# A new hand-written order of all engines: first-layer weights in whole quarters, and 53 fills of 256 columns

## The chip, the cores and the metric

One Trainium2 chip, and one of its cores. A core has a tensor engine (PE; its weight loads are listed apart as PEld), a vector engine (DVE), a scalar engine (ACT), a pool engine (POOL) and a sync engine whose queue (SP) issues all DMAs of this kernel. The metric is the device time of one execution in microseconds, lower is better. The kernel before took 179.84 us, the median of 179.12, 179.84 and 180.20.

## The reference

A gated linear recurrence over 768 steps for 4 batches and 8 heads of 48 dimensions, and behind it two dense layers over the 3072 tokens.

```python
f = 1 / (1 + exp(-f_logit))
for t in range(S):                                   # S = 768
    state = f[:, :, t, :, None] * state + einsum('bhd,bhe->bhde', k[:, :, t], v[:, :, t])
    y[:, :, t] = einsum('bhd,bhde->bhe', q[:, :, t], state)
x = y.transpose(0, 2, 1, 3).reshape(3072, 384)
h = x @ w_in                                         # 384 x 2048
out = maximum(0.01 * h, h) @ w_out                   # 2048 x 384
```

## The kernel before, in words

The sequence is cut into chunks of 128 steps. The work comes in 12 units: units 0 to 3 hold chunks 0 and 1 of one batch each, and units 4 to 11 hold one later chunk of two batches each. `a` is the half of a unit (a group of heads in units 0 to 3, a batch in the others; 2 means both).

A unit runs through the parts below. The names are the words of the order, `name_unit_a`, and the last number of some words names the engine (0 DVE, 1 ACT or POOL, 2 POOL).

- `Lf Lk Lq Lv` load f_logit, k, q and v on SP's queue. `ge` (line 229) takes an exponential of the gate logits on ACT and `gl` (line 241) the logarithm, which gives `lf`.
- `cs` (lines 250 to 261) makes the cumulative sums of `lf` with matmuls against triangular masks; `ca` (line 266, DVE) finishes them for two units. `dec` (lines 274 to 280, ACT) turns them into the three decay factors `em`, `at` and `end`.
- `k` and `q` (line 286) scale the keys and queries, and `v` (lines 291 to 300, POOL) casts the values. `tk tq` transpose on PE (line 319) and `ck cq` copy the result out (lines 332, 334); from unit 3 on `xk xq` transpose by DMA instead (line 339).
- `sc` (lines 355, 362) makes the scores, `mk` (lines 372, 376, DVE) masks them, and `mx` and `ms` (line 393) mix values and states into the output. `xt` (lines 445, 447) copies that into `xT`, the input of the first layer.
- `pt` (lines 458, 463) makes a chunk's contribution to the state, `sf` (lines 473, 475, DVE) adds it, and `sb` (lines 480, 483, POOL) scales and casts the state.
- `up` (line 510, for one unit, 6 matmuls of 256 columns) and `uw` (line 521, for two units, 3 matmuls of 512 columns) are the first layer; `pr` and `pw` (lines 516, 525, ACT) its leaky relu into `gT`. `dn` (line 532, 4 matmuls of 384 columns) is a quarter of the second layer for 128 tokens; `dh` (line 548) is the same layer for half of the columns. `ob` and `oh` copy out, `st` and `sh` store.

The weights come as four quarters each. `WI_i` (line 173) loads 512 columns of the first layer's weights into a staging tile, and `CI_i_x` (lines 200, 202) casts one of its three slices of contraction rows. `We_i_x` (line 180) loads only 256 of the columns, and `Ce_i_x_y` (lines 187, 189) casts 128 of those. `WO` and `CO` do the same for the second layer. The staging tiles are the raw tiles of units 4 and 5, and a `WO_i` uses the staging tile of `WI_i`.

`F_n@b` (line 134) issues n matmuls of a constant tile into PSUM bank b. Nothing reads them.

Nothing is scheduled by a compiler. The string `order` near the end lists every part with the PSUM banks it uses, and each engine and the queue run their own words in the order of that string. There are 8 banks, so a word on PE also waits until the reader of the bank's last contents is done.

Of the kernel before, what the change touches and what calls it, by code (L numbers as in the profile page):

```python
# [15 lines left out]
def kernel(  # L16
# [10 lines left out]
    nc = tc.nc  # L27
# [53 lines left out]
    banks = [psum.tile([128, 512], FP32, name=f"ps{i}", tag=f"ps{i}") for i in range(8)]  # L81
# [4 lines left out]
    ut = const.tile([128, 128], BF16, tag="ut")  # L86
# [3 lines left out]
    filler = const.tile([128, 128], BF16, tag="filler")  # L90
# [41 lines left out]
    def fill(n, bank):  # L132
        for _ in range(n):
            nc.tensor.matmul(banks[bank].rearrange("t (a n) -> t a n", a=4), filler,  # L134
                             filler[:, None, :].to_broadcast([128, 4, 128]), start=True, stop=True)
# [349 lines left out]
    def wide(j):  # L485
        return j // 2 * 2 in WIDE
# [101 lines left out]
    sc_0_0@6.2 q_1_1_1 zv_1_1 mk_0_0_0 gl_2_1 F_2@1 cs_2_1@3 q_1_0_0 ca_2_1 F_1@4 tq_1_0@1 dec_2_0 ck_1_0_0 cq_1_0_1
    mk_0_0_1 tq_1_1@4 We_0_0 q_2_0_0 cq_1_1_1 v_1_0 dec_2_1 Lv_2_2 WI_2 F_2@5 sc_1_0@6.7 mx_0_2@5.1 sc_1_1@2.4
    mk_1_0_1 mk_1_0_0 v_1_1 tq_2_0@7 q_2_1_1 mk_1_1_1 mk_1_1_0 xt_0_0_1 ms_0 pt_1_2@3.6 xt_0_1_1 Ce_0_1_0_1  # L590
    Ce_0_1_1_1 F_2@2 mx_1_2@5.4 k_2_0_0 tk_2_0@1 sf_1_0 cq_2_0_0 Ce_0_0_0_1 Ce_0_0_1_1 xt_1_0_1 up_0_1@2 k_2_1_1
    ck_2_0_0 sb_1_0 tq_2_1@3 tk_2_1@7 sf_0_1 v_2_1 v_2_0 We_1_0 up_0_0@1 cq_2_1_1 CI_2_1_2 zs_2_1 ms_1 pr_0_1
    xt_1_1_1 ut Ce_1_0_0_2 ck_2_1_0 sc_2_0@5.0 sc_2_1@3.7 sf_1_1 pr_0_0 mk_2_1_0 CI_2_0_1 pt_2_2@2.6 CI_2_2_0
    up_1_1@4 mk_2_0_1 sf_2_0 up_1_0@1 mk_2_1_1 Ce_1_0_1_1 pr_1_1 pr_1_0 mk_2_0_0 up_0_5@3 up_1_5@0 We_1_1 Lf_3_2
    sb_2_0 WI_3 up_1_4@2 up_0_2@4 mx_2_2@7.1 WO_0 CI_3_1_2 ms_2 xt_2_1_0 Ce_1_1_1_0 xt_2_0_1 up_1_2@5 up_0_4@7
    Ce_1_1_0_0 pr_1_5 pr_1_2 WO_2 pr_1_4 CI_3_2_2 zs_3_0 ge_3_0 pr_0_2 WO_1 up_0_3@1 ge_3_1 CI_3_0_0 up_2_3@0
    up_2_1@5 up_1_3@2 pr_0_3 sf_2_1 up_1_6@4 gl_3_0 pr_1_3 up_0_6@6 up_2_0@1 pr_0_5 CO_0_1_0 CO_0_2_0 pr_2_3 up_2_2@2
    up_2_7@3 sb_0_1 cs_3_0@0 CO_0_0_2 CO_2_1_2 pr_0_4 CO_2_0_2 gl_3_1 CO_1_2_2 Lf_4_1 CO_1_0_2 pr_2_1 pr_2_2 pr_0_6
    ca_3_0 cs_3_1@7 dec_3_0 pr_2_7 pr_1_6 dn_0_1_0@5 up_2_4@2 up_1_7@6 dn_0_0_0@0 up_2_6@3 Lk_3_2 dn_1_0_0@4 CO_1_1_2
    Lf_5_1 pr_2_4 k_3_0_0 CO_2_2_0 ca_3_1 dec_3_1 Lq_3_2 Lf_5_0 WO_3 dn_0_0_1 q_3_1_1 pr_2_6 CO_3_1_0 k_3_1_1 Lf_4_0  # L600
    dn_1_0_1 dn_1_0_2 dn_0_1_1 dn_1_1_0@2 dn_0_0_2 Lv_3_2 dn_1_1_1 xk_3 sb_1_1 pr_1_7 dn_1_1_2 up_2_5@7 q_3_0_0
    dn_0_1_2 up_0_7@3 CO_3_0_0 v_3_0 sb_2_1 CO_3_2_1 pr_0_7 xq_3 Lq_4_0 v_3_1 Lk_4_0 Lq_5_1 Lk_5_1 Lk_5_0 Lq_5_0
# [78 lines left out]
```

## Time and profile before

| | us |
|---|---|
| median of three runs | 179.84 |
| the profiled execution, its own time | 178.5 |
| its span, first to last instruction | 176.7 |
| its last matmul ends at | 173.8 |
| PE busy | 168.0 |
| ACT busy | 107.5 |
| DVE busy | 79.1 |
| POOL busy | 72.7 |

Times in the text count from the start of the span. The profile of an engine says when an instruction ran, and what ended the idle time before it. A matmul's listed duration holds its latency; in a row of matmuls the next one starts earlier, so what a group costs PE is read from the chain of waits, which lists starts and merged lengths.

### The profile page before, as it was taken

To read this page: it belongs to the slowest core of one execution; us is meant where nothing else is said; L and a number is where in the kernel's file an instruction comes from. 1 tells how busy PE (TensorE), PEld (TensorE's weight loads), DVE (VectorE), ACT (ScalarE), POOL (GpSimd) and SP (SyncE) were. 2 spreads that over 40 slices of the span, in tenths; PEclk is the share of its full clock that TensorE was granted. 3 is DMA by queue.
4 is the path that set the end of the run, shared out by engine and by line. 5 is a ranking of instruction groups with operands and counts; after the bars stand their busy time and mean duration, and the time that the engine had idled before them with its cause. 6 is when DMAs were issued, how large, how long until landed. Compare 5 with 4: busy or idle time off the path is not lost.

```text
span 176.7 us, 5136 instructions
## 1 busy us (share of the span) xinstructions
PE 168.0 (95%) x2096; PEld 105.6 (60%) x2096; DVE 79.1 (45%) x166; ACT 107.5 (61%) x234; POOL 72.7 (41%) x151
## 2 busy tenths in 40 slices
PE   7698889999999999999999998999999999999993
PEld 2475668787566786754556744455754555644662
DVE  5259957802217333835128844506735355300030
ACT  4886964999155599269960687641799610378401
POOL 4687585532551745208525344802206980000000
PEclk9999999999999999999999999999999999999999
DMA  5999999499999499979999889999999990103004
GB/s 148 317 323 342 355 312 353 125 326 209 312 206 210 91 194 177 215 188 200 211 229 233 192 188 216 227 134 212 264 206 225 156 250 0 48 0 137 0 22 156
DMA packets 110407, 34.93 MB, mean 198 GB/s; under 512 B 102832, under 2 KB 109616, under 8 KB 110384
## 3 DMA queue, kind: packets, MB, share of 16 engines
q1 hardware_dynamic: 110384, 34.61, 84.1%
q8 instruction: 16, 0.26, 0.6%
q14 instruction: 7, 0.06, 0.1%
HBM read 25.17 MB, written 4.72 MB: 169 GB/s over the span
## 4 chain that ended last, share of the span: by engine, by line
PE 90%; DVE 3%; ACT 2%; DMA 2%; issue 1%; SPq 0%; DVEq 0%
PE ps L532 35%; PE ps L521 22%; PE ps L510 11%; PE ps L393 6%; PE ps L134 3%; PE ps L362 3%; DMA raw_fk<-in_f_logit_dram 2%; PE ps L319 2%; PE ps L548 2%; PE ps L258 1%; DVE wm L372 1%; PE ps L463 1%; PE ps L355 1%; PE ps L458 1%; PE ps L250 1%
## 5 line engine op out<-in xcount | busy, mean ns | idle before, releaser
L532 PE MATMUL ps<-w_out,gT 128*128 128x384 bf16 x368 | 66.1, 326 | 0.9 <-DVE sf L475 0.9
L532 PEld LDWEIGHTS <-gT 128*128 128x128 bf16 x368 | 34.4, 98 | 24.3 <-issue 1.2
L521 PE MATMUL ps<-xT,w_in 128*128 128x512 bf16 x192 | 45.2, 379 | 0.0
L525 ACT ACTIVATE gT<-ps 128x512 bf16<-128x512 f32 x64 | 34.5, 623 | 10.1 <-PE ps L521 9.6
L521 PEld LDWEIGHTS <-w_in 128*128 128x128 bf16 x192 | 18.1, 98 | 18.9
L376 DVE TENSOR_TENSOR wm<-ps,ut 128x512 bf16<-128x512 f32 x32 | 19.9, 684 | 17.0 <-PE ps L362 12.2
L286 POOL TENSOR_TENSOR qh<-raw_qv,at 128x768 bf16<-128x768 f32 (+1 forms) x10 | 14.0, 1404 | 24.3 <-ACT gT L525 9.4
L510 PE MATMUL ps<-xT,w_in 128*128 128x256 bf16 x192 | 22.9, 273 | 0.4 <-ACT xT L445 0.2
L516 ACT ACTIVATE gT<-ps 128x512 bf16<-128x512 f32 x32 | 17.9, 616 | 6.2 <-PE ps L510 6.2
L291 POOL CAST vb<-raw_qv 128x384 bf16<-128x384 f32 (+1 forms) x16 | 11.6, 723 | 23.6 <-DMA raw_qv<-in_v_dram 23.4
L510 PEld LDWEIGHTS <-w_in 128*128 128x128 bf16 x192 | 18.4, 98 | 3.6 <-DVE w_in L189 0.5
L483 POOL CAST sb<-sf 64x192 bf16<-64x192 f32 x40 | 14.9, 374 | 10.8 <-DVE sf L473 8.5
L445 ACT CAST xT<-ps 128x384 bf16<-128x384 f32 x15 | 7.8, 529 | 16.9 <-PE ps L393 13.5
L274 ACT ACTIVATE em<-ps 128x384 bf16<-128x384 f32 x24 | 12.2, 508 | 9.0 <-DVE wm L376 5.5
L229 ACT ACTIVATE e<-raw_fk 128x384 f32<-128x384 f32 (+1 forms) x16 | 11.0, 685 | 8.1 <-DMA raw_fk<-in_f_logit_dram 8.0
L286 DVE TENSOR_TENSOR kh<-raw_fk,em 128x768 bf16<-128x768 f32 (+1 forms) x10 | 9.0, 901 | 14.6 <-ACT em L274 9.7
L475 DVE TENSOR_TENSOR sf<-sf,ps 64x192 f32<-64x192 f32 x32 | 11.2, 351 | 6.4 <-ACT at L275 2.8
L543 DVE COPY osb<-ps 128x384 f32<-128x384 f32 x13 | 7.1, 554 | 13.0 <-PE ps L532 9.0
L275 ACT ACTIVATE at<-ps 128x384 bf16<-128x384 f32 x24 | 12.3, 512 | 0.0
L480 POOL TENSOR_TENSOR sf<-sf,end 128x192 f32<-128x192 f32 x16 | 8.9, 556 | 5.9 <-DVE sf L475 5.6
L372 DVE TENSOR_TENSOR wm<-ps,pair_mask 128x512 bf16<-128x512 f32 x16 | 10.4, 685 | 1.8 <-ACT lf L241 0.9
L134 PE MATMUL ps<-filler 128*128 128x512 bf16 x24 | 9.2, 511 | 2.0 <-DVE filler L93 1.1
(90 smaller groups left out, 180.2 us busy)
## 6 DMA issues: line engine op xcount, KB each, us to landing
out_dram<-osb SPq DMA_DIRECT2D x23, 192.0 KB, 3.1
raw_fk<-in_f_logit_dram SPq DMA_DIRECT2D x18, 192.0 KB, 3.8
raw_qv<-in_v_dram SPq DMA_DIRECT2D x18, 192.0 KB, 3.6
raw_fk<-in_k_dram SPq DMA_DIRECT2D x18, 192.0 KB, 3.7
raw_qv<-in_q_dram SPq DMA_DIRECT2D x18, 192.0 KB, 3.8
raw_fk<-in_moe_w_out_dram SPq DMA_DIRECT2D x2, 768.0 KB, 7.2
raw_qv<-in_moe_w_out_dram SPq DMA_DIRECT2D x2, 768.0 KB, 5.0
raw_fk<-in_f_logit_dram SPq DMA_DIRECT2D x3, 384.0 KB, 4.7
```

The costliest lines, as they stand in the source:

```text
L134: nc.tensor.matmul(banks[bank].rearrange("t (a n) -> t a n", a=4), filler, filler[:, None, :].to_broadcast([128, 4, 128]), start=True, sto ...
L274: nc.scalar.activation(ems[j % 2][:, a], t[:, 0:H * D], AF.Exp, scale=1.0)
L275: nc.scalar.activation(ats[j % 2][:, a], t[:, 0:H * D], AF.Exp, scale=-1.0)
L286: eng.tensor_mul(heads(j, to[j % NR], a)[:, :, :, 0:D], raw_heads(j, x, a), decays(j, by, a))
L372: nc.vector.tensor_mul(w.rearrange("t (s p) n -> t s p n", s=2), src.rearrange("t (s p n) -> t s p n", s=2, p=2), pair_mask[:, :, None, :] ...
L376: nc.vector.tensor_mul(w, src.rearrange("t (p n) -> t p n", p=P2), ut[:, None, :].to_broadcast([128, P2, 128]))
L483: nc.gpsimd.tensor_copy(out=sb[rows, :, y * D:y * D + D], in_=sf[rows])
L510: nc.tensor.matmul(pm[:, i, :], w_in_of(ff, kk), xTs[j // 2 % 2][:, kk, j % 2].rearrange("t a s -> t (a s)"), start=(kk == 0), stop=(kk == ...
L516: nc.scalar.activation(dst, pm, AF.Prelu, alpha=0.01)
L521: nc.tensor.matmul(banks[bank], w_in_of(ff, kk), xTs[j // 2 % 2][:, kk].rearrange("t u a s -> t (u a s)"), start=(kk == 0), stop=(kk == NK ...
L525: nc.scalar.activation(g_blocks(j)[ff], banks[st[j].pop(("pm", ff))], AF.Prelu, alpha=0.01)
L532: nc.tensor.matmul(po, g_of(j, ff, a), w_out_b[quarter][:, ff % 4, :], start=(ff == 0), stop=(ff == NF - 1))
```

## The change

Three things change. The fill matmul has 256 columns instead of 512. The order string is another one from its first line to its last, so all engines and SP's queue run their words in a new sequence, with other banks. Some parts change their engine or their form: the first-layer weights are loaded as `WI_0` to `WI_3` and cast by `CI` (four loads of 768 KB, where there were two of these and four `We` of half the size), and 11 places in the order hold 53 fills, where 8 places held 24. All other matmuls are the same ones as before.

```diff
     def fill(n, bank):
         for _ in range(n):
-            nc.tensor.matmul(banks[bank].rearrange("t (a n) -> t a n", a=4), filler,
-                             filler[:, None, :].to_broadcast([128, 4, 128]), start=True, stop=True)
+            nc.tensor.matmul(banks[bank][:, 0:256].rearrange("t (a n) -> t a n", a=2), filler,
+                             filler[:, None, :].to_broadcast([128, 2, 128]), start=True, stop=True)
...
     order = """
-    c0 Lf_0_1 ge_0_1 Lf_1_2 ge_1_1 gl_0_1 ge_1_0 zk_0 zv_0_0 zs_0_0 Lv_0_1 Lf_0_0 F_7@1 cs_0_1@0 ge_0_0 gl_0_0 Lk_0_1
+    c0 Lf_0_1 zs_1_1 zk_2 ge_0_1 zk_0 Lk_0_1 Lf_0_0 Lq_0_0 Lf_1_2 Lk_0_0 Lq_0_1 gl_0_1 F_16@1 cs_0_1@0 zs_0_1 ge_0_0
...
```

PE's words in the new order, as far as the first two `up`, are `F_16@1 cs_0_1 F_1@2 cs_0_0 F_19@3 cs_1_0 tq_0_1 tk_0_1 cs_1_1 tk_0_0 tq_0_0 F_1@3 sc_0_1 tq_1_0 F_1@6 sc_0_0 pt_0 tk_1_0 F_4@1 tq_1_1 sc_1_0 tk_1_1 cs_2_0 F_2@6 sc_1_1 F_3@1 pt_1 cs_2_1 mx_0 F_2@4 mx_1 ms_0 ms_1 cs_3_1 cs_3_0 up_0_1 tq_2_0 up_0_0`. Behind them come `F_1@5` and `F_3@4` between ups. Before, PE began with `F_7@1 cs_0_1 F_3@2 cs_0_0 F_3@3 cs_1_0`, and had four more fill places ahead of its second `mx`.

The first place is ACT at the start of the program. `e` is the exponential of one half of a unit's gate logits (line 229; tile 76 is unit 0, 77 is unit 1), `lf` its logarithm, and `em`, `at`, `end` are the decay factors. Before:

```order
L229 ACTIVATE e_76<-raw_fk_64 128x384
L229 ACTIVATE e_77<-raw_fk_65 128x384
L241 ACTIVATE lf_78<-e_76 128x4x2x48
L229 ACTIVATE e_77<-raw_fk_65 128x384
L229 ACTIVATE e_76<-raw_fk_64 128x384
L241 ACTIVATE lf_78<-e_76 128x4x2x48
L274 ACTIVATE em_87<-ps_155 128x384
```

Now:

```order
L229 ACTIVATE e_76<-raw_fk_64 128x384
L241 ACTIVATE lf_78<-e_76 128x4x2x48
L229 ACTIVATE e_76<-raw_fk_64 128x384
L241 ACTIVATE lf_78<-e_76 128x4x2x48
L274 ACTIVATE em_87<-ps_155 128x384
L275 ACTIVATE at_89<-ps_155 128x384
L277 ACTIVATE end_91<-ps_155 128x2x2
```

The logarithm of unit 0's first half stood behind an exponential of unit 1, which needs unit 1's load; now it follows its own exponential, and all of unit 0's gate stands ahead of unit 1.

The second place is SP's queue where the first-layer weights are loaded. `raw_fk_66` and `raw_qv_72` are unit 2, `raw_fk_67` is unit 3, and tiles 68, 69, 74 and 75 are the staging of quarters 0, 2, 1 and 3. Before:

```order
L164 DMA raw_fk_66<-in_k_dram 128x8x96
L180 DMA raw_fk_68<-in_moe_w_in_dram 128x3x256 x2
L164 DMA raw_qv_72<-in_v_dram 128x8x96
L173 DMA raw_fk_69<-in_moe_w_in_dram 128x3x512
L180 DMA raw_qv_74<-in_moe_w_in_dram 128x3x256 x2
L164 DMA raw_fk_67<-in_f_logit_dram 128x8x96
L173 DMA raw_qv_75<-in_moe_w_in_dram 128x3x512
```

Now:

```order
L164 DMA raw_fk_67<-in_f_logit_dram 128x8x96
L173 DMA raw_fk_68<-in_moe_w_in_dram 128x3x512
L164 DMA raw_qv_72<-in_q_dram 128x8x96
L173 DMA raw_fk_69<-in_moe_w_in_dram 128x3x512
L164 DMA raw_fk_66<-in_k_dram 128x8x96
L173 DMA raw_qv_74<-in_moe_w_in_dram 128x3x512
L173 DMA raw_qv_75<-in_moe_w_in_dram 128x3x512
L164 DMA raw_qv_72<-in_v_dram 128x8x96
```

Unit 3's gate logits moved ahead of all weights, and unit 2's q and k behind quarter 0 and quarter 2.

The third place is DVE between the masks of unit 2 and the state of unit 2 (`xT_126` is unit 2's input to the first layer, `w_in_172` is quarter 1, `sb` are state tiles being cleared). Before:

```order
L372 TENSOR_TENSOR wm_108<-ps_162,pair_mask 128x512
L372 TENSOR_TENSOR wm_105<-ps_160,pair_mask 128x512
L447 CAST xT_126<-ps_156 128x3x2x64
L189 CAST w_in_172<-raw_qv_74 128x3x128 x2
L127 MEMSET sb_0_123 128x192
```

Now:

```order
L123 MEMSET v_100 128x8x16
L334 COPY qT_103<-ps_159 128x2x256
L202 CAST w_in_172<-raw_qv_74 128x512
L334 COPY qT_103<-ps_158 128x2x256
L334 COPY kT_101<-ps_156 128x2x256
L334 COPY kT_101<-ps_162 128x2x256
L202 CAST w_in_174<-raw_qv_75 128x512
L372 TENSOR_TENSOR wm_105<-ps_162,pair_mask 128x512
```

The cast of quarter 1 stood behind unit 2's masks and behind the copy of unit 2's output; now it stands ahead of unit 2's masks.

More of the change, by code (lines that the diff above doesn't have):

```diff
@@ L588 @@
[L588 to L602, printed above, removed]
@@ new lines @@
+    cs_2_1@1 ca_2_1 ge_3_1 ge_3_0 sb_1_0 gl_3_1 gl_3_0 dec_2_0 CI_0_2_1 CI_0_0_2 mx_0_2@2.6 zs_2_0 xt_0_0_0 F_2@4
+    mx_1_2@4.5 ms_0 ms_1 cs_3_1@3 xt_0_1_1 dec_2_1 q_2_0_1 CI_0_1_0 cs_3_0@2 xt_1_0_0 xt_1_1_1 ca_3_1 up_0_1@6 pr_0_1
+    ca_3_0 tq_2_0@4 up_0_0@1 sf_0_1 up_1_1@5 WI_3 sf_1_1 CI_2_1_1 CI_2_2_0 ut dec_3_1 q_2_1_0 Lv_2_2 CI_2_0_2 k_2_1_0
+    up_1_0@7 up_1_5@6 up_0_5@0 k_2_0_0 zv_2_0 pr_0_0 pr_1_1 pr_0_5 CI_1_2_2 tq_2_1@3 cq_2_0_0 WO_0 pr_1_0 F_1@5
+    tk_2_1@1 up_0_4@5 up_1_4@0 Lk_3_2 tk_2_0@7 CI_1_1_1 dec_3_0 pr_1_5 CI_1_0_0 CI_3_2_2 cq_2_1_0 v_2_1 F_3@4
@@ L646 @@
+    sh_11_1_0
     """
```

103 lines of the change are left out of this document (56 added, 47 removed).

## The prediction

> **What bounds the kernel now.** I read the page first, then the busy time by stage, then the chain of waits.
>
> ```profile
> span 176.7 us, 5136 instructions
> PE 168.0 (95%) x2096; PEld 105.6 (60%) x2096; DVE 79.1 (45%) x166; ACT 107.5 (61%) x234; POOL 72.7 (41%) x151
> PE 90%; DVE 3%; ACT 2%; DMA 2%; issue 1%; SPq 0%; DVEq 0%
> ```
>
> PE is the bound: it has 90% of the chain. A gain can come only from holes on PE, from matmuls at a low rate and from fills. The stages show where those lie (stretch, length, busy us of PE, PEld, DVE, ACT, POOL, granted clock, DMA share, GB/s).
>
> ```profile
> 0.00:5.80 5.80, 3.17 (x8) 1.04 (x9) 2.40 (x15) 2.79 (x5) 2.25 (x17) 1.00 0.72 186
> 5.80:22.17 16.37, 15.02 (x338) 10.30 (x337) 12.47 (x27) 13.85 (x37) 12.62 (x31) 1.00 1.14 335
> 22.17:33.05 10.88, 10.02 (x208) 7.93 (x205) 7.26 (x18) 6.41 (x13) 7.51 (x21) 1.00 0.92 308
> 33.05:107.00 73.95, 73.95 (x905) 48.88 (x906) 32.90 (x67) 49.36 (x109) 31.95 (x53) 1.00 0.96 206
> 107.00:111.00 4.00, 3.08 (x21) 1.40 (x18) 1.81 (x4) 3.23 (x9) 1.24 (x4) 1.00 1.13 224
> 111.00:173.80 62.80, 62.76 (x627) 36.05 (x625) 22.29 (x38) 31.51 (x66) 17.14 (x28) 1.00 0.64 133
> ```
>
> From 33.05 to 173.80 PE has one hole, 0.92 us in the row 107 to 111. What else can be won lies ahead of 33 us. The chain of waits shows it (start, length, what).
>
> ```profile
> 1.26 3.53 DMA raw_fk<-in_f_logit_dram
> ...
> 5.33 0.42 ACT lf L241
> 5.80 0.32 PE ps L250
> 6.68 1.30 PE ps L134 x3
> 8.71 1.29 PE ps L134 x3
> ...
> 12.66 0.86 PE ps L134 x4
> ...
> 18.02 0.74 PE ps L393 x61
> ...
> 22.03 0.60 ACT xT L445
> ...
> 22.67 0.70 PE ps L510 x5
> ...
> 23.43 0.45 issue
> ...
> 31.59 0.28 DVE xT L447
> 31.88 0.21 issue
> 32.09 0.91 DVE w_in L189 x2
> 33.05 6.07 PE ps L510 x54
> ```
>
> The first real matmul waits until 5.80 for a logarithm that stands behind another unit's load. And matmuls run at half rate until about 9.8: a fill of 512 columns costs 0.43 us at 6.68 and 8.71 and 0.215 at 12.66, though the granted clock reads 1.00 throughout. A fill of 256 columns is put at 0.215 and 0.108 accordingly.
>
> **The start, up to the third cumulative sum.** ACT's prices are the distances from start to start in the timeline.
>
> ```profile
> 3.43 0.52 ACT L229 ACTIVATE e<-raw_fk 128x384 f32<-128x384 f32 x1 [1.42 <-DMA raw_fk<-in_f_logit_dram]
> 4.81 0.52 ACT L229 ACTIVATE e<-raw_fk 128x384 f32<-128x384 f32 x1 [0.86 <-DMA raw_fk<-in_f_logit_dram]
> 5.24 0.51 ACT L241 ACTIVATE lf<-e 128x384 bf16<-128x384 f32 x1
> 11.32 0.49 ACT L274 ACTIVATE em<-ps 128x384 bf16<-128x384 f32 x1
> 12.14 0.54 ACT L229 ACTIVATE e<-raw_fk 128x384 f32<-128x384 f32 x1
> 16.92 1.07 ACT L332 COPY qT<-ps 128x512 bf16<-128x512 bf16 x2 [0.74 <-PE ps L319]
> ...
> 35.88 2.06 ACT L516 ACTIVATE gT<-ps 128x512 bf16<-128x512 f32 x4 [0.34 <-PE ps L510]
> ```
>
> A gate step takes 0.43 (4.81 to 5.24), a set of decays 0.82 (11.32 to 12.14), a transposed copy 0.535, a relu 0.52. Unit 0's first load is not moved, so the exponential starts at 3.43 again; its logarithm now follows at 3.86 and ends at 4.37. The 16 fills last from 1.05 to 1.05 + 16 x 0.215 = 4.49, and `cs_0_1` starts there instead of at 5.80. The other half of unit 0 has 576 KB loaded up to and with it, as much as the load that ended at 4.79 before (1.26 + 3.53). Its logarithm ends near 5.75, and `cs_0_0` runs from 5.8 to 6.7 (0.88, as 5.80 to 6.68). F_19 then costs 19 x 0.108 = 2.05 at full rate, to 8.75, or 4.1 at half rate, to 10.8. ACT needs until about 9.4 for what follows `cs_0_0` (decays of unit 0's second half from 6.85, then four gate steps of unit 1), so at full rate F_19 fills a real wait and costs nothing. I take full rate from about 6.5 on, since PE is busy from 1.05 almost without a break, where before it stood still from 4.1 to 5.8 and the rate doubled some 4 us after that.
>
> [...]
>
> **Up to the first first-layer matmul.** From 9.4 on ACT's queue holds, ahead of the copy that completes unit 0's `xT`, three sets of decays, six copies, eight gate steps and one weight cast: 3 x 0.82 + 6 x 0.535 + 8 x 0.43 + 0.5 = 9.6, so 19.0 with no wait at all, and 19.6 with that copy (0.60). On PE the chain goes over POOL's cast of unit 1's values.
>
> ```profile
> 15.52 0.50 POOL L291 CAST vb<-raw_qv 128x384 bf16<-128x384 f32 x1 [0.77 <-DMA raw_qv<-in_v_dram]
> 16.65 0.50 POOL L291 CAST vb<-raw_qv 128x384 bf16<-128x384 f32 x1
> 21.41 0.81 POOL L483 CAST sb<-sf 64x192 bf16<-64x192 f32 x2 [0.76 <-DVE sf L473]
> ```
>
> Unit 1's values are the queue's 13th transfer now and were its 14th, with 384 KB less ahead of them, some 1.1 us at 335 GB/s. The load ended at 15.5, so now at 14.4. Two casts of 1.1 each (15.52 to 16.65) and the state cast of 0.8 between them end at 17.4. Then `pt_1` and `cs_2_1` (0.45 and 0.24 in the same chain view), both `mx` (0.74 each, the row at 18.02), two fills and `ms_0` (0.28) end at 20.1, and the copy at 20.7. This chain is the longer one; its ten handovers are counted at nothing and may cost up to 0.1 each, and its loads may be 0.3 earlier. I take the first `up` at 21.0, bounds 20.4 to 21.7, against 22.17. At that point PE has done 0.26 more: `ms_1` and both `cs_3` (0.28 and 2 x 0.24), less two transposes of unit 2 (2 x 0.25). Whole quarter 0 is 4608 KB into the queue, by 335 GB/s near 17, so its casts are not what is waited for. **Gain 1.4, bounds 0.7 to 2.0.**
>
> **From the first `up` to 33 us.** PE waited here from 22.17 to 22.67 but for one matmul of 0.1 (0.4), then 0.45, then from 31.59 to 33.05 (1.46): 2.3 in all. In the largest the copy of unit 2's output stood on DVE ahead of the two casts of quarter 1. That row of DVE is now ahead of unit 2's masks, and the cast follows the load. What it adds: four fills (0.43) among the ups, and waits of PE for banks, where ACT needs 14 x 0.52 for relus, 4 x 0.5 for casts and 2 x 0.82 for decays, 10.9 of some 13.5 us. I put these waits at 0.8, between 0.2 and 1.9. **Gain 2.3 - 0.43 - 0.8 = 1.1, bounds 0 to 1.7.**
>
> **Behind 33 us.** The order of everything else changes too, with the same matmuls. The one hole before was a bank that DVE's state addition had to free (columns as in the chain above).
>
> ```profile
> 110.08 0.34 DVE sf L475
> 110.46 0.37 DVE sf L475
> 110.87 0.81 PE ps L532 x4
> ```
>
> In the new order I find banks that come free only 0.1 to 0.5 us ahead of their next use, in each of the four wide units. I expect waits of about the same 0.9 us there: gain 0, bounds a gain of 0.9 and a loss of 3. The tail, two half layers and a store, is the same: nothing.
>
> **The sum.** -1.4 - 1.1 + 0 = -2.5 against the profiled execution's 178.5 (span 176.7 and 1.8 around it), so 176.0. That execution is 1.3 below the median; the same difference off the median gives **177.3**. With all bounds at their best it is 179.84 - 4.6 = 175.2, and at their worst 179.84 - 0.7 + 3 = 182.1.
>
> **Rivals.** (1) *The half rate lasts until 9.9 again.* F_19 then ends at 10.8, `cs_1_0` is 2.0 late, and ACT, which has unit 1's decays in front of all its copies, passes that on: -2.5 + 2.0, 179.3. For it speaks that this execution doubled only then; against it the pause before 5.80, which is gone.
>
> (2) *The middle is held by the loads.* The DMA share is 0.96 from 33 to 107 and 1.13 behind it. If loads cannot come earlier, PE's lead melts into waits: 179.8. Against it: the weights of the second layer wait for casts less often now, and the queue stood still for 4.9 and 3.6 us ahead of two of them.
>
> ```profile
> SPq L192 <- DVE w_in L189: 4.9, 1, 4.9
> SPq L192 <- DVE w_in L202: 3.6, 1, 3.6
> ```
>
> (3) *Slower: values behind the transposes.* On SP the values of units 6 and 7 stand behind unit 7's two DMA transposes, and POOL casts both in turn just ahead of PE's `mx_7`. Before, POOL waited longest of all for such loads, and PE's `mx` began at 98.4, with the second cast running.
>
> ```profile
> POOL vb L291 <- DMA raw_qv<-in_v_dram: 23.4, 8, 7.4
> 97.93 0.82 POOL L291 CAST vb<-raw_qv 128x768 bf16<-128x768 f32 x1 [1.32 <-DMA raw_qv<-in_v_dram]
> ```
>
> By my count of the queue the cast ends 0.8 us ahead of `mx_7` now. What the loads are late beyond that is lost one for one, since all ups of the pair wait for it. It makes the kernel slower from 0.8 + 2.5 + 0.9 = 4.2 us on; at 5.1 it is 181.6. The single wait of 7.4 shows that such a size occurs; that it never held PE before speaks against it.
>
> **Chances.** Forecast 0.60, (1) 0.12, (2) 0.08, (3) 0.20. A measurement can tell about 0.5% from no change, that is 178.9 to 180.7. The forecast lies below that, a third of (1) too: faster 0.64; the rest of (1) and (2) same: 0.14; (3) slower: 0.22, with a little of (2). The range is 175.0 to 181.4; the forecast's own is 175.2 to 178.9.
>
> **What would show it.** Right: the first line 250 matmul near 4.5, fills of 256 columns at 0.108 in the row of 19, the first line 510 matmul between 20.4 and 21.7, no wait of over 0.5 us for `w_in`, and PE busy through the rest but for 1 us. Wrong: the row of 19 fills lasting 4 us (1); the third `cs` waiting for a load; PE idle in front of line 393 with POOL's line 291 as the releaser (3), or more than 2 us of holes behind 33 us from ACT.

## The result: slower by 3.8%

| | before | after |
|---|---|---|
| median, us | 179.48 (178.87 to 180.20, 4 runs) | 184.99 (184.28 to 185.28, 4 runs) |
| the profiled execution | 178.5 | 185.28 |
| its span | 176.7 | 183.5 |
| its mean granted clock | 1.000 | 0.972 |

The ratio is 1.0382, with a 95% interval of 1.0328 to 1.0437. The forecast was 177.3, with a range of 175.0 to 181.4. Here and below, a ratio compares those executions of each kernel that lie within 1.5% of its fastest; a time given as measured is the median of all.

The page of the changed kernel first: the span, PE's busy time, the granted clock in 40 slices, and a DMA queue that the prediction never looked at (pieces, MB, share of the engines).

```profile
span 183.5 us, 5178 instructions
PE 171.7 (94%) x2125; PEld 110.2 (60%) x2125; DVE 84.4 (46%) x176; ACT 107.3 (58%) x233; POOL 68.4 (37%) x140
PEclk9999685899999999999999999999999999999999
q8 instruction: 16, 0.26, 0.5%
```

PE is busy 3.7 us longer than before, with only 29 matmuls more, and the clock row has a dent at 6, 8 and 5 where before it had 9 throughout. The busy time by stage shows where (columns as in the prediction).

```profile
10.00:15.00 5.00, 3.96 (x87) 2.88 (x85) 3.54 (x8) 4.04 (x12) 3.85 (x9) 1.00 1.05 285
15.00:20.00 5.00, 3.71 (x97) 2.62 (x105) 4.39 (x10) 4.49 (x11) 3.21 (x10) 0.97 0.97 301
20.00:25.00 5.00, 2.67 (x131) 1.68 (x109) 2.39 (x7) 1.09 (x4) 3.22 (x7) 0.69 1.08 368
25.00:30.00 5.00, 3.82 (x50) 2.88 (x50) 3.75 (x10) 3.14 (x8) 1.42 (x2) 0.66 1.07 371
30.00:35.00 5.00, 5.00 (x36) 3.83 (x35) 1.47 (x5) 2.18 (x6) 2.57 (x8) 0.66 0.87 286
35.00:107.00 72.00, 71.34 (x945) 48.03 (x946) 38.75 (x70) 43.97 (x94) 24.80 (x47) 1.00 0.98 189
107.00:180.40 73.40, 73.32 (x764) 42.04 (x752) 26.79 (x50) 41.47 (x88) 23.60 (x37) 1.00 0.67 146
```

Before, in the same three stretches from 20 us on:

```profile
20.00:25.00 5.00, 3.82 (x98) 2.64 (x92) 3.75 (x11) 3.31 (x8) 4.05 (x12) 1.00 1.03 315
25.00:30.00 5.00, 5.00 (x95) 4.33 (x95) 4.11 (x9) 3.35 (x7) 2.54 (x8) 1.00 1.01 360
30.00:35.00 5.00, 4.82 (x110) 3.80 (x109) 3.39 (x10) 3.80 (x9) 3.39 (x7) 1.00 0.57 159
```

Behind 35 us PE is full but for 0.7 us, so all of the loss lies ahead of it. Two things are new there: a stretch in which PE does little (2.67 of 5 us from 20 to 25), and a clock of 0.66 from 25 to 35. (The counts of 36 and 110 matmuls from 30 to 35 do not compare: 76 of the 110 are small ones of line 393.) What the clock costs is seen on rows of one kind: 30 first-layer matmuls take 5.42 us in the chain below, 0.18 each, and 54 took 6.07 before, 0.11 each. The chain of waits names the first.

```profile
18.54 0.51 POOL vb L291
19.09 0.35 PE ps L458 x8
19.79 1.06 PE ps L393 x54
20.84 0.54 PE ps L134 x2
21.39 1.29 PE ps L393 x63
22.67 2.49 issue
25.16 0.36 PE ps L393 x10
25.55 0.59 ACT xT L445
26.95 0.48 ACT xT L445
27.47 1.22 PE ps L510 x5
29.12 5.42 PE ps L510 x30
```

For 2.49 us in the middle of `ms_0` PE waits for "issue", that is, for nothing that the profile shows. In the chain of before the same word stands at 23.43, with 0.45 us. I counted the rows of PE's program, one for each matmul and one for each weight load: **both executions stop behind row 703, though at another instruction in each.** In the queue "instruction" a piece of 16 KB (0.26 MB in 16) ran from 22.77 to 23.73 in the changed kernel and PE went on at 25.16; before it ran from 21.63 to 22.59 and PE went on at 23.88. I read this as: PE had run out of program, and the next piece came late. From the first of the 16 pieces to the last, PE went on by 3717 rows in the changed kernel (13.91 to 159.32 us) and by 3750 before (14.98 to 160.10), 248 and 250 to a piece. I count 256 rows to a piece, an estimate: the power of two next to these; kernels of 4184 to 4276 rows had 16 pieces, and those of 4280 to 4346 had 17.

The second, the clock, changes at 19.73, 23.14, 26.55 and 33.38 us, in steps of 3.41 us or twice that; a window below is such a stretch of 3.41. The stages cut at its own steps:

```profile
16.32:19.73 3.41, 2.24 (x54) 1.44 (x52) 2.89 (x7) 2.90 (x8) 2.35 (x8) 1.00 0.91 284
19.73:23.14 3.41, 2.94 (x135) 1.95 (x133) 2.63 (x8) 1.36 (x5) 2.59 (x6) 0.50 1.11 372
23.14:26.55 3.41, 1.29 (x35) 1.01 (x35) 0.43 (x2) 1.00 (x3) 0.69 (x2) 1.00 1.05 377
26.55:29.97 3.42, 2.50 (x14) 1.85 (x14) 3.29 (x9) 2.11 (x6) 1.39 (x2) 0.50 1.07 358
29.97:33.38 3.41, 3.41 (x18) 2.35 (x16) 1.36 (x4) 1.79 (x5) 2.60 (x8) 0.50 1.08 346
```

The three half-rate windows stand behind windows in which PE was busy for 2.24 us, for 1.29 (the stop) and for 2.50. Together they are 10.2 us.

### The profile page after: what moved, and what is told of

It reads as the page before. It is cut to its first block, busy times and chain, and to the rows that moved or that the text cites. A ratio compares the mean times of both kernels' runs of the same rounds, so it can differ in the third digit from the quotient of the medians.

```text
span 183.5 us, 5178 instructions
## 1 busy us (share of the span) xinstructions
PE 171.7 (94%) x2125; PEld 110.2 (60%) x2125; DVE 84.4 (46%) x176; ACT 107.3 (58%) x233; POOL 68.4 (37%) x140
## 4 chain that ended last, share of the span: by engine, by line
PE 83%; DMA 6%; SPq 3%; issue 3%; POOL 2%; ACT 1%; POOLq 0%
PE ps L532 31%; PE ps L521 23%; PE ps L510 13%; PE ps L393 6%; SPq L164 3%; DMA raw_fk<-in_k_dram 3%; DMA qT<-qh 3%; PE ps L362 2%; PE ps L258 1%; PE ps L548 1%; PE ps L463 1%; POOL kh L286 1%; PE ps L458 1%; PE ps L355 1%; PE ps L319 1%
## 5 line engine op out<-in xcount | busy, mean ns | idle before, releaser
L521 PE MATMUL ps<-xT,w_in 128*128 128x512 bf16 x192 | 44.5, 379 | 0.0
L525 ACT ACTIVATE gT<-ps 128x512 bf16<-128x512 f32 x64 | 35.9, 632 | 12.1 <-PE ps L521 12.0
L521 PEld LDWEIGHTS <-w_in 128*128 128x128 bf16 x192 | 18.1, 98 | 19.3
L510 PE MATMUL ps<-xT,w_in 128*128 128x256 bf16 x192 | 25.8, 292 | 1.0 <-ACT xT L445 1.0
L516 ACT ACTIVATE gT<-ps 128x512 bf16<-128x512 f32 x32 | 17.9, 627 | 10.7 <-PE ps L510 10.7
L510 PEld LDWEIGHTS <-w_in 128*128 128x128 bf16 x192 | 19.7, 104 | 5.4 <-issue 1.2
L543 DVE COPY osb<-ps 128x384 f32<-128x384 f32 x12 | 6.6, 556 | 31.2 <-PE ps L532 28.4
L291 POOL CAST vb<-raw_qv 128x384 bf16<-128x384 f32 (+1 forms) x16 | 10.6, 664 | 26.7 <-DMA raw_qv<-in_v_dram 21.1
L480 POOL TENSOR_TENSOR sf<-sf,end 128x192 f32<-128x192 f32 x16 | 9.4, 587 | 22.0 <-DVE sf L475 21.5
L286 POOL TENSOR_TENSOR qh<-raw_qv,at 128x384 bf16<-128x384 f32 (+1 forms) x8 | 11.2, 1405 | 11.5 <-ACT at L275 4.2
L445 ACT CAST xT<-ps 128x384 bf16<-128x384 f32 x10 | 5.3, 529 | 14.3 <-PE ps L393 14.0
L286 DVE TENSOR_TENSOR qh<-raw_qv,at 128x384 bf16<-128x384 f32 (+1 forms) x8 | 7.4, 928 | 10.9 <-DMA raw_qv<-in_q_dram 10.8
```

Source lines behind the costliest of these rows:

```text
L286: eng.tensor_mul(heads(j, to[j % NR], a)[:, :, :, 0:D], raw_heads(j, x, a), decays(j, by, a))
L510: nc.tensor.matmul(pm[:, i, :], w_in_of(ff, kk), xTs[j // 2 % 2][:, kk, j % 2].rearrange("t a s -> t (a s)"), start=(kk == 0), stop=(kk == ...
L516: nc.scalar.activation(dst, pm, AF.Prelu, alpha=0.01)
L521: nc.tensor.matmul(banks[bank], w_in_of(ff, kk), xTs[j // 2 % 2][:, kk].rearrange("t u a s -> t (u a s)"), start=(kk == 0), stop=(kk == NK ...
L525: nc.scalar.activation(g_blocks(j)[ff], banks[st[j].pop(("pm", ff))], AF.Prelu, alpha=0.01)
```

## The experiments

The theories, as the expectations name them. **R**: PE stops behind row 703 for a late piece of its program. **C**: the loss comes from the half clock that follows PE's idling. **F**: the narrow fills cost by themselves. **L**: the stop is a wait for a certain load or value. **D** and **B**, on why the piece is late: it stands behind large weight packets, or behind bytes of any kind. The line numbers of an experiment are shifted by the lines that its edit adds.

**1. The new order with wide fills.**

```diff
     def fill(n, bank):
-        for _ in range(n):
+        for i in range(n // 2):
+            nc.tensor.matmul(banks[bank].rearrange("t (a n) -> t a n", a=4), filler,
+                             filler[:, None, :].to_broadcast([128, 4, 128]), start=True, stop=True)
+        if n % 2:
             nc.tensor.matmul(banks[bank][:, 0:256].rearrange("t (a n) -> t a n", a=2), filler,
                              filler[:, None, :].to_broadcast([128, 2, 128]), start=True, stop=True)
```

> The new order, with its fills in 512 columns again and half as many (same columns, 22 matmuls and so 44 rows of PE's program fewer ahead of the hole). Theory R (PE stands still after the 703rd row of its program, for a 16 KB piece of the instruction stream that lands late): the hole stays, but moves to another instruction, to whatever is row 703 now (line 393 or 250 some 44 rows further on), 1.5 to 2.5 us long; 183.5 to 185.5 us. Theory F (the form of the fills is what costs): 179.5 to 181. Theory L (the hole is a wait for one particular load or value): the hole stays at the same matmul of line 393; 184.5 to 185.5.

Measured: 181.66, ratio 1.0207 (1.0147 to 1.0267). PE's timeline at the stop (start, length, instruction, idle time before it):

```profile
24.93 0.24 PE L253 MATMUL ps<-lf,bu 128*128 128x192 bf16 x1 [4.43 <-issue]
```

The stop stays behind row 703 and moves to the instruction that is now next, a cumulative sum: R, not L. It is longer than R said, 4.43 us: the piece left later (4.26 us after row 416, where the changed kernel has 3.64) and PE got there earlier (2.22 us after that row instead of 3.25). Yet the time lies 1.8 us below R's range (and 0.7 above F's), 1.7% below the changed kernel by the two ratios: only one window at half clock followed (25.29 to 28.70), where the changed kernel had three. So the two parts of the loss can go apart. The rest of the new order, with wide fills, still costs 2.1%.

**2. More rows at the start.**

```diff
+    def fill_small(n, bank):
+        for _ in range(n):
+            nc.tensor.matmul(banks[bank][0:32, 0:64], filler[:, 0:32], filler[:, 0:64], start=True, stop=True)
...
-F_16@1
+f_64@1
```

> The new order; the first 16 fills of 256 columns become 64 fills of 64 columns with 32 columns of weights: as many columns, 96 more rows of PE's program at the very start. Theory R: the request for the next piece goes out 96 rows earlier, near 16.5 us instead of 19.7, while the matmuls that need it stand where they stood; the hole of 2.49 us shrinks below 0.5, the first matmul of line 510 comes near 23.7 instead of 26.19, and the window after 26.5 runs at full clock: 179.5 to 181.5 us. Theory C (all follows from the clock, which falls because PE idles between 16.3 and 19.7): the half rate from 19.7 on is as before; 183 to 185. Theory L: hole unchanged, 184.5 to 185.5.

Measured: 183.19, ratio 1.0283 (1.0239 to 1.0327). Two timeline rows, the 19 fills and the stop:

```profile
7.16 3.58 PE L134 MATMUL ps<-filler 128*128 128x256 bf16 x19
22.59 0.29 PE L397 MATMUL ps<-wm,v 64*32 64x128 bf16 x9 [2.16 <-issue]
```

Again behind row 703, again in another place. It did not shrink below 0.5: PE comes to that row at 20.21 instead of 22.39 us, and the piece began only at 20.26. The clock doubled at 9.96 us, 3.89 later than in the changed kernel, so that the 19 fills took 3.58 instead of 2.23 us; whether for the small fills or for the place at which the windows fell, one trace does not tell. The time lies in C's range, but the half-rate windows (23.61 to 30.44) follow the stop, and the one from 19.7 that C expected is not there. As a way to lift the stop this failed; that the stop goes with the row stands.

**3. PE kept busy ahead of the states of unit 1.**

```diff
-F_2@6 ... F_3@1 pt_1_2
+F_5@6 ... F_13@1 pt_1_2
```

> The new order with 13 more fills of 256 columns ahead of the last scores and the states of unit 1, so that PE does not idle between 16.5 and 19.1 us but for what a matmul inside the states waits. Theory C: the granted clock stays 1.00 from 19.7 to 23.1, and the time falls by 1.5 or more: 181 to 183.5 us. Theory R: the clock may hold there, but the hole stays (2 to 3 us, 26 rows earlier in the program) and with it the half rate behind 26.5; 184 to 186.

Measured: 183.93, ratio 1.025 (1.0138 to 1.0363). The stages at the clock's steps, and the stop in the timeline:

```profile
18.79:22.20 3.41, 3.16 (x148) 2.34 (x146) 2.50 (x8) 2.57 (x8) 2.42 (x7) 1.00 1.01 331
22.20:25.61 3.41, 1.49 (x48) 1.18 (x48) 1.87 (x4) 0.85 (x3) 1.66 (x4) 1.00 1.08 368
25.61:29.02 3.41, 2.40 (x15) 1.73 (x14) 3.28 (x9) 2.10 (x7) 1.02 (x1) 0.50 1.08 373
```

```profile
24.12 0.31 PE L393 MATMUL ps<-wm,v 64*32 64x128 bf16 x11 [2.17 <-issue]
```

As C said, the first half-rate window is gone; as R said, the stop is there and the windows behind it too. The time lies between the two ranges. Both theories hold, each for its part.

**4. The head of before, the rest of the new order.** The words of before up to the last second-layer word of unit 0 (`dn_0_1_3`, near 55 us), then all words of the new order that were not yet done.

> The order of before (with its fills) up to the last down projection of unit 0, near 55 us, then the rest in the new order. If the whole loss lies in the first 37 us: 178.8 to 180.3, as before. If the new order also costs something further on: 181 or more. If it wins there: below 178.5.

Measured: 181.33, ratio 1.0101 (1.0035 to 1.0168), which rests on four of seven executions; the other three took 182.06 to 182.71 at a mean clock of 0.991. The profiled execution took 180.28. At the seam PE waits 2.41 us, since ACT has a load and an exponential in front of the decays it needs:

```profile
62.41 0.32 PE L258 MATMUL ps<-lf,ut 128*128 128x384 bf16 x1 [2.41 <-ACT end L280]
```

That seam is of the splice and in neither kernel, and its 2.41 us are more than the 1.8 by which the run is slower (1.01%). So nothing speaks for a loss in the new order behind 55 us.

**5. The weights in small packets.**

```diff
     def load_w_in(i):
-        nc.sync.dma_start(out=staging(i).rearrange("t (k n) -> t k n", k=NK),
-                          in_=moe_w_in[:, 512 * i:512 * i + 512].rearrange("(k p) n -> p k n", p=128))
+        for x in range(4):
+            at = 512 * i + 128 * x
+            nc.sync.dma_start(out=staging(i).rearrange("t (k n) -> t k n", k=NK)[:, :, 128 * x:128 * x + 128],
+                              in_=moe_w_in[:, at:at + 128].rearrange("(k p) n -> p k n", p=128))
```

> The new order, with each quarter of the first-layer weights loaded by four transfers of 128 columns (packets of 512 bytes) instead of one of 512 columns (packets of 2 KB); the same bytes at the same place of the queue. Theory D (the instruction piece comes late because it stands behind large weight packets in the DMA engines): the second piece starts no more than 2.5 us after PE has passed row 416, against 3.6, the hole after row 703 shrinks from 2.49 to 1.3 or less; 181.5 to 183.5 us. Theory B (it stands behind bytes, of whatever packet): hole 2.2 to 2.8, 184.5 to 186. Both keep the stop after row 703.

```profile
22.99 0.51 PE L394 MATMUL ps<-qT,sb 128*32 128x128 bf16 x22 [0.55 <-issue]
```

The piece left 1.96 us after row 416 and the stop shrank from 2.49 to 0.55: D, not B. The four executions took 178.53, 181.40, 181.97 and 182.46 us at mean clocks of 0.998, 0.990, 0.978 and 0.981. A ratio would rest on the first alone and is not given. In the profiled one (181.97) two windows still ran at half clock: one behind a window with the wait inside unit 1's states (0.93 us; PE busy for 2.07 of 3.41), which this run leaves as it was, and one behind a window with the stop and a wait of 1.01 us for `xT` (busy for 1.85).

**6. No weight loads.** The `WI` words are left out, and the casts of the first-layer weights read unit 0's raw tile, so that layer multiplies by other numbers.

```diff
     def cast_w(to):
...
-            dst, src = to[i].rearrange("t k n -> t (k n)")[:, cols], staging(i)[:, cols]
+            held = raw_fk[0].rearrange("t x a h d -> t (x a h d)") if to is w_in_b else staging(i)
+            dst, src = to[i].rearrange("t k n -> t (k n)")[:, cols], held[:, cols]
```

> The new order with the loads of the first-layer weights left out: the casts read unit 0's raw tile in their place, so the first layer multiplies by other numbers; 3 MB less are moved ahead of 30 us, and everything else stands. Theories D and B: the second piece starts within 2 us of row 416 and the hole after row 703 is below 0.8; the granted clock then stays full behind 26.5; 177 to 181 us. If the piece always takes 3 to 4 us, whatever else is moved: the hole stays at 2 or more, 183 to 185.

One execution: 179.74, clock 1.00, the piece 1.88 us after row 416, as D and B said. The stop is 1.50 us, which neither said: PE reached row 703 at 20.24 instead of 22.39, ahead of a piece that ended at 20.69.

**7. Wide fills and small packets**: the edits of 1 and 5 together.

> The new order with both: fills of 512 columns, half as many (as in the first experiment, 181.66 with a hole of 4.5 us after row 703), and the weights in packets of 512 bytes. Theory D: the hole shrinks by 1.5 to 3 us: 178.5 to 180.5. Theory B: hole 4 or more, 181 to 182.5.

Measured: 178.01, 180.97, 181.01 and 181.06 us, no ratio, for the same reason as in 5. The piece left 2.00 us after row 416 and the stop shrank from 4.50 to 2.17 (start to start). D's sign, and less than it said of the time.

**8. The narrow fills alone, in the order of before.** The fill of the changed kernel, and twice as many at each of the eight places (three up to the third cumulative sum and five behind it, all ahead of row 703):

```diff
-F_7@1 F_3@2 F_3@3 F_4@5 F_2@1 F_1@4 F_2@5 F_2@2
+F_14@1 F_6@2 F_6@3 F_8@5 F_4@1 F_2@4 F_4@5 F_4@2
```

> The order of before, its 24 fills of 512 columns as 48 of 256: the change's new form of fills alone. Theory R: 48 rows more of PE's program lie ahead, row 703 is reached some 0.8 us earlier and the hole after it grows by up to that (0.67 from start to start before): 178.5 to 180.5 us. Theory F (narrow fills themselves keep the array less busy and lower the clock): 181 or more, the clock below 1.00 somewhere ahead of 25 us.

Measured: 183.63, ratio 1.0275 (1.0198 to 1.0352). The stop and the stages at the clock's steps:

```profile
24.64 0.43 PE L393 MATMUL ps<-wm,v 64*32 64x128 bf16 x13 [2.52 <-issue]
```

```profile
20.50:23.91 3.41, 1.22 (x55) 0.82 (x55) 1.86 (x5) 1.71 (x5) 2.45 (x8) 1.00 1.05 353
23.91:27.32 3.41, 2.68 (x28) 1.95 (x28) 1.13 (x3) 0.59 (x1) 2.44 (x8) 0.50 1.08 360
27.32:30.74 3.42, 3.42 (x64) 2.40 (x63) 1.13 (x3) 2.19 (x5) 0.00 (x0) 0.50 0.60 218
```

This is the run that says most. **The form of the fills alone, with not one word moved, costs 2.75%; the whole change costs 3.82%.** The two don't simply add up, since the new order with wide fills costs 2.1% (run 1). The stop of 0.45 us grew to 2.52, and two half-rate windows follow it. I had sized its growth at 0.8 us; rows 416 to 703 took 1.30 us less (4.89 to 3.59 in the table below) and the piece was 0.5 later, and the clock was not in the sum. The time and the clock, which falls at 23.91 us, are those that F named, and not R's. But the window ahead of that step (20.50 to 23.91, PE busy for 1.22 us) holds most of the stop, and run 11 tells the two apart.

**9. Three remedies in the new order**: the small packets of 5, the 13 fills of 3, and `F_19@3` as 38 fills of 128 columns.

```diff
-F_19@3 ... F_2@6 ... F_3@1
+f_38@3 ... F_5@6 ... F_13@1
...
+    def fill_128(n, bank):
+        for _ in range(n):
+            nc.tensor.matmul(banks[bank][:, 0:128], filler, filler, start=True, stop=True)
```

> The new order with three things at once: weights in packets of 512 bytes; the row of 19 fills as 38 of 128 columns (the same time, 38 more rows of PE's program early, so that the second piece is requested earlier in a place with fewer matmuls); 13 more fills of 256 columns where PE idled between 16.5 and 19.1 us. Theories R, D and C together: no hole over 0.5 us after row 703, no window at half clock between 10 and 30 us in most runs: 177.5 to 179 us. If one of the three is not what costs: a hole of 1 us or more there, or half windows, and 180.5 to 183.

Measured: 179.90, ratio 1.0071 (1.0025 to 1.0118). The time is 0.9 above the range. No half-rate window in the profiled execution, but six of the twelve executions had a mean clock of 0.991 or less; a stop of 0.70 us was left, not below 0.5.

**10. Small packets in the order of before** (there also for the loads by halves, two transfers of 128 columns each).

```diff
     def load_w_in_half(i, x):
-        nc.sync.dma_start(out=half_of(staging(i).rearrange("t (k n) -> t k n", k=NK), x),
...
+        for y in range(2):
+            at = 256 * x + 128 * y
+            nc.sync.dma_start(out=staging(i).rearrange("t (k n) -> t k n", k=NK)[:, :, at:at + 128],
...
```

> The order and fills of before, all first-layer weights in packets of 512 bytes. Theory D: the second piece starts about 2 us after row 416 (3.3 before), the stop of 0.45 us after row 703 goes: 0.3 to 1 us faster than before. If small packets slow the weights themselves: PE waits longer for casts of weights around 30 us, and the kernel is 0.5 to 2 us slower.

Measured: 179.26, ratio 0.9973 (0.9916 to 1.0031), from six of twelve executions. PE no longer stops behind row 703, but what it won there (0.45 us) can't be told from nothing.

**11. Narrow fills and small packets in the order of before**: the edits of 8 and 10.

> The order of before with 48 fills of 256 columns (183.6 with a hole of 2.7 us after row 703) and the weights in packets of 512 bytes. Theories R and D: the hole shrinks to 1.2 or less, 179 to 181.5. If the narrow fills cost through something other than the late piece: 183 or more.

Measured: 180.37, ratio 1.0070 (1.0019 to 1.0122), clock 1.00 in the profiled execution (0.99 or less in five of ten), a stop of 0.86. Small packets take three quarters of what the narrow fills cost in 8, though in 10 they win nothing by themselves: that part went through the late piece and the clock behind it, and not through the narrow fills as such, as F had it.

**12. Unit 1's values earlier.** The edits of 9 without the 13 fills, and `Lv_1_2` ahead of `Lf_2_2`.

```diff
-Lf_2_2 v_0_1 ... Lv_1_2
+Lv_1_2 Lf_2_2 v_0_1
```

> The new order, weights in packets of 512 bytes, the row of 19 fills as 38 of 128 columns, and unit 1's values loaded ahead of unit 2's gates (one place earlier by 384 KB, 1.1 us) instead of more fills. If the wait inside unit 1's states was for these values: it shrinks from 0.85 us to below 0.2, no hole over 0.5 us after row 703, the first matmul of line 510 by 24 us: 177.5 to 179.5. If the gates of unit 2 become the wait instead: the cumulative sums of unit 2 come 0.5 to 1 later and nothing is gained over the run with 13 more fills.

Measured: 181.29, ratio 1.0173 (1.0095 to 1.0252). The wait of 0.85 us inside the states is gone, but a wait of 0.76 stands ahead of the scores, the stop is 1.40 us, and in the profiled execution the start fell in a half-rate window (7.52 to 10.93 us). It settles little.

**13. Three moves in the order of before**, with small packets.

```diff
-ge_1_1 gl_0_1             xt_2_1_0 Ce_1_1_1_0 ... Ce_1_1_0_0     k_8_2_0 sf_7_1
+gl_0_1 ge_1_1             Ce_1_1_1_0 Ce_1_1_0_0 xt_2_1_0         sf_7_1 k_8_2_0
```

> The order and fills of before with the weights in packets of 512 bytes, and four words moved, each to take away a wait that the traces of before or of the run with packets alone show: unit 0's first logarithm ahead of unit 1's exponential (the first cumulative sum at 4.4 us instead of 5.8), the two casts of the second half of quarter 1 ahead of unit 2's output copy on DVE (a wait of 0.65 near 32 us), the state addition of unit 7 ahead of unit 8's scaled keys on DVE (a wait of 0.9 to 1.2 near 109 us). If PE's holes are what is left to win: 177 to 178.3 us, 0.5 to 1.2% faster than before. If the start is held by the loads anyway and the holes only move: 178.5 to 180.

Measured: medians 178.95 against 179.26 of before. The ratio given, 0.9857 (0.9774 to 0.9940), rests on two of six executions, so I don't call it faster. PE's timeline shows what became of the early start:

```profile
4.54 0.27 PE L253 MATMUL ps<-lf,bu 128*128 128x192 bf16 x1 [0.31 <-ACT lf L244]
7.49 0.24 PE L253 MATMUL ps<-lf,bu 128*128 128x192 bf16 x1 [1.69 <-ACT lf L244]
```

The first cumulative sum comes at 4.54, and the second then waits 1.69 us for a logarithm that follows a load.

**14. Small packets and the 13 fills in the new order**, without the 38 narrow ones.

> The new order, weights in packets of 512 bytes, and the 13 more fills of 256 columns between 16.5 and 19.1 us, without the 38 narrow ones. Theory C (with the hole small, what is left of the loss are windows at half clock that follow PE's idling between 16.3 and 19.5): most runs at a clock above 0.995 and 178.5 to 180.5 us, against 178.5 to 182.5 with packets alone. If the clock falls in most runs in spite of the fills: 181 to 183.

Measured: 180.10, ratio 1.0020 (0.9980 to 1.0060), over 11 of 12 executions; eight of the twelve had a clock above 0.995. The stages at the clock's steps:

```profile
16.18:19.59 3.41, 3.41 (x115) 2.73 (x115) 2.75 (x6) 3.41 (x10) 1.55 (x5) 1.00 1.08 293
19.59:23.00 3.41, 2.70 (x122) 1.89 (x110) 3.13 (x8) 0.98 (x4) 2.32 (x5) 1.00 1.08 300
23.00:26.42 3.42, 2.40 (x25) 2.15 (x24) 3.29 (x10) 2.63 (x8) 0.61 (x1) 1.00 1.06 299
```

Between the doubling at 5.94 us and the last matmul no stage falls to half rate. **With the piece earlier and PE busy, the new order takes as long as before, to within 0.6%: the loss of 3.8% is gone.** A stop of 0.71 us is left. The interval of run 10, the order of before with the same packets, overlaps with this one.

**15. Only the two moves on DVE of run 13**, with small packets.

> As the run with three moves, but without the early logarithm: the order and fills of before, weights in packets of 512 bytes, the two casts of quarter 1 ahead of unit 2's output copy and unit 7's state addition ahead of unit 8's scaled keys. If the two waits on DVE (0.65 and 0.9 to 1.2 us) were real losses: 177.3 to 178.6 us, 0.5 to 1% faster than before, and no worse than with the early logarithm. If PE only waits elsewhere instead: 178.5 to 179.8, as before.

Measured: 178.29 against 179.19, ratio 0.9965 (0.9926 to 1.0004), over ten of twelve executions. Both waits are gone from the trace: PE has no hole near 32 us, and its largest behind 33 us is 0.17 us. By the two ratios to before that is 4.0% below the changed kernel (0.9965 / 1.0382). Against before it is 0.35% less, which the interval just does not tell from nothing. The early start of run 13 adds nothing that could be seen.

The pieces side by side, from the trace of each run. Row 416 is a mark: count PE's rows in groups of 256, and the earliest piece of a trace, against its group, began behind row 140 to 167 in all 17 traces. So I take it that the second piece, the one with row 704, is asked for near row 256 + 160.

| kernel | packets of `w_in` | PE from row 416 to 703, us | second piece starts after row 416, us | PE's stop behind row 703, start to start |
|---|---|---|---|---|
| before | 2 KB, 1 KB | 4.89 | 3.30 | 0.67 |
| after | 2 KB | 3.25 | 3.64 | 2.78 |
| 1 | 2 KB | 2.22 | 4.26 | 4.50 |
| 2 | 2 KB | 4.33 | 4.38 | 2.38 |
| 3 | 2 KB | 2.77 | 2.72 | 2.39 |
| 4 | 2 KB, 1 KB | 4.90 | 4.33 | 1.67 |
| 8 | 2 KB, 1 KB | 3.59 | 3.79 | 2.74 |
| 6 | not loaded | 2.38 | 1.88 | 1.73 |
| 5 | 512 B | 3.53 | 1.96 | 0.78 |
| 7 | 512 B | 2.24 | 2.00 | 2.17 |
| 9 | 512 B | 3.91 | 2.50 | 0.92 |
| 11 | 512 B | 3.59 | 2.19 | 1.07 |
| 12 | 512 B | 2.88 | 2.17 | 1.62 |
| 14 | 512 B | 2.77 | 1.26 | 0.92 |
| 10 | 512 B | 4.90 | 1.80 | none |
| 13 | 512 B | 6.06 | 1.74 | none |
| 15 | 512 B | 4.89 | 2.66 | 0.21 |

Where PE does not stop there, row 704 starts 0.05 to 0.06 us after row 703 (runs 10 and 13); the 0.21 of run 15 is a small stop too. The piece itself takes about 1 us (0.96 before and in the changed kernel), and wherever PE had stopped it went on 1.3 to 1.5 us after the piece's end. So I estimate that PE needs some 2.4 us beyond the delay: where rows 416 to 703 took longer than the delay and these 2.4 together, nothing is seen; where they took less, PE lost the difference (in the changed kernel 3.64 + 2.4 - 3.25 = 2.8), to within 0.2 us in every row of the table. With 2 KB packets the delay is 2.7 to 4.4 us, with 512 bytes 1.3 to 2.7.

D agrees with the table in sign; that the piece waits behind the large packets themselves is the theory's reading, and no run shows it. (A packet in this text is what the profile lists as one, a single row.)

## Why the prediction was wrong, point by point

In short: the sum put the stop behind row 703 at nothing (2.49 us measured), and it priced every matmul behind the start at the full rate (10.2 us ran at half). A gain of 2.5 us became a loss of 5.5.

**The start** was right in its first step and of no use. `cs_0_1` began at 4.48 (4.49 predicted), the rate doubled at 6.07 (6.5 predicted) and F_19 took 2.23 us (2.05). But the second half came later than the 5.8 taken:

```profile
4.48 0.33 PE L250 MATMUL ps<-lf,bu 128*128 128x192 bf16 x1
6.66 0.24 PE L250 MATMUL ps<-lf,bu 128*128 128x192 bf16 x1 [1.05 <-ACT lf L241]
7.09 2.23 PE L134 MATMUL ps<-filler 128*128 128x256 bf16 x19
```

The text went by bytes, 576 KB ahead of either load. But on SP's queue this load is the third one issued, at 1.79 us, where the one that it was compared with was the second, at 1.26. From issue to exponential the two took about the same, 3.74 and 3.55 us (to 5.53 and 4.81). The 6.5 was an estimate from one execution, and that the unbroken row of fills set the moment is not shown: run 15, with PE's first words as before, has the clock's first step at 4.84. Run 13 shows the same in the order of before: an earlier first sum only lengthens the wait for the next load.

**Up to the first first-layer matmul** the prediction said 21.0, bounds 20.4 to 21.7; it was 26.19, and the row of them began at 27.47. Two terms of this step failed. The values of unit 1 were put at 14.4 by a queue of 335 GB/s, and POOL got them at 16.92:

```profile
16.92 0.50 POOL L291 CAST vb<-raw_qv 128x384 bf16<-128x384 f32 x1 [1.12 <-DMA raw_qv<-in_v_dram]
```

The queue moved 285 GB/s from 10 to 15 us. But the price was also one row of one execution. In the order of before, where this cast began at 15.52, the runs have it between 15.32 (run 10) and 16.93 us (run 15); in the new order it begins between 14.96 (run 14) and 17.13 (run 3). The 1.1 us that the sum took off is less than this scatter; why the start scatters stays open. The rest, 2.49 us, is the stop behind row 703, a term that the sum put at nothing. (Two smaller misses cancel: POOL's casts took 2.13 us instead of 3.0, and PE's part behind them some 1.0 more than counted, since it ran in the half-rate window from 19.73 us, with 1.06 for an `mx` instead of 0.74.) I had quoted the row of that stop in the chain of before, "23.43 0.45 issue", and counted it among the holes that the new order would close, without asking what PE was waiting for.

**The price of the fills** was taken by columns alone: half as wide, half the time. That was right (0.108 us each at full rate), and it left out that each fill is two rows of PE's program, narrow or wide: line 134 has 24 matmuls and 24 weight loads before, 53 and 53 in the changed kernel. Run 8 shows what that is worth in the order of before: 2.75%.

**From the first `up` to 33 us** a gain of 1.1 was expected, bounds 0 to 1.7. The waits named there did shrink: before lost 2.3 us, the changed kernel 1.01 us for `xT` and nothing for weights. But the step, like the whole sum, priced matmuls at the rate that the start had reached, and the rate fell: 6.83 us at half clock from 26.55 on. There the row of 30 matmuls took 5.42 us, 0.18 each. The text weighed the clock at the start only, as rival (1).

**Behind 33 us** the step was right: one hole, 0.63 us at 79 us (0.92 before, bounds of a gain of 0.9 and a loss of 3). Rival (3), the values behind the transposes, did not come, and rival (2) neither. None of the rivals was the mechanism that decided; "slower" had a chance of 0.22, but for another reason.

**What remains of the expected gain** is told in part by run 14: with the stop small and without the half clock the new order ties with before, where 1.4% less was expected. There unit 1's values came in time (the cast began at 14.96 without a wait), and still the first `up` began at 22.77 and the row of them at 24.05, 1.4 later than before. Its chain of waits holds 1.52 us of the fills that this run adds, 0.71 of the stop, and 1.9 us on ACT (two copies to `xT` with a set of decays between them). So run 14 does not show what the new order would take without its stop and without added fills. The two executions of runs 5 and 7 that kept a clock of 0.998 or more took 178.53 and 178.01, beside a median of 178.67 for before, measured along with them: no run of the new order shows the 1.4%.

How the loss divides is shown only in part. Packets and fills together take all of it away (14). Fills alone, against the first half-rate window, leave 2.5% (3). Wide fills in the new order leave 2.1% (1). Packets alone leave a time that goes with the clock, 178.5 to 182.5 (5).

## What to carry to other kernels

A row called "issue" in front of PE is worth a look at the queue of instruction loads: count PE's rows to the stop, and see whether it stays behind the same row while the work ahead of it is changed, as it did here in 15 of 17 traces. Instructions added ahead of it can move the stop to other work and widen it, filler too: 24 more fills took it from 0.67 to 2.74 us (run 8, start to start). Loading with smaller packets at that time helped here (2.78 to 0.78 in run 5); whether keeping rows of cheap matmuls apart from large transfers does so too, no run tried. And price a hole on PE by the clock that follows it as well as by its length: in the changed kernel 6.83 us at half clock followed the stop of 2.49.

## What the runs showed of the hardware

**PE's program came in pieces of 16 KB.** The changed kernel and the one before have 16 of them, 248 and 250 rows apart on the mean. In 15 of the 17 traces PE stops behind row 703 exactly, for 0.21 to 4.50 us from start to start and at eight different places of the work; in the other two (runs 10 and 13) the piece had ended 1.7 us or more before PE came to that row.

**The clock fell to half behind windows in which PE was busy, too.** The half-rate stretches of the changed kernel last 3.41 and 6.83 us, and PE's busy time is taken in windows of 3.41 us from the clock's first step on. At full clock every window with PE busy for less than 1.5 us was followed by one at half clock (0.35 in run 1, 1.49 in run 3), and none with 2.28 (run 5) or more was. Between them both occurred: 1.60 (run 7) and 2.24 us (the changed kernel) were followed by half, 1.51 (run 4, in the seam from 60.51 us) and 1.98 (run 4, from 22.96) by full. So busy time alone does not settle it. At half clock, windows busy for 2.40 (run 3) to 2.78 us (run 2) stayed at half, and those with 2.94 (the changed kernel) or more went back to full.

The windows do not start with the kernel: in the five traces that begin in the order of before with wide fills (before, 4, 10, 13 and 15), the clock's first step stands at 9.86, 9.31, 10.46, 4.62 and 4.84 us, which is 3.03, 2.48, 0.22, 1.21 and 1.43 us into a grid of 3.41. The same program had mean clocks from 0.978 to 0.998 (run 5), and its time moved by 3.9 us; that this comes from the place of the windows fits, but was not shown.
